# V cast while it is loaded, one clamp per half batch, first decay rows by small DMAs, and products in four 32-column tiles

## The chip, the cores and the metric

The kernel runs on one core of one Trainium2 chip. The metric is the device time in microseconds (us). TensorE (PE) multiplies, VectorE (DVE), ScalarE (ACT) and GpSimd (POOL) compute elementwise, SyncE (SP) only issues DMAs here; ACT and POOL issue some too.

## The reference

Eight batches of eight heads, 576 positions, head size 64; an attention with a decay (forget gate f), and after it a feed-forward net with a gated convolution along the sequence:

```python
log_f = np.log(np.clip(f, 0.0001, 1.0))
cum = np.cumsum(log_f, axis=-1)
scores = q @ k.T / sqrt(64) + cum[i] - cum[j]        # causal: j <= i
attn = softmax(scores);  x = attn @ v                # x: [8, 576, 512], heads side by side
h = relu(x @ w_in)                                   # [576, 1024]
conv = w0 * h[s-1] + w1 * h[s] + w2 * h[s+1]         # per channel
out = (h * sigmoid(conv)) @ w_out                    # [576, 512]
```

All inputs are fp32.

## The kernel before

A **half batch** (`hb`, 16 of them) is four heads. `load_qk` brings its q and k with a transposing DMA that treats each fp32 as two 16-bit numbers, so that the tile `qk` (four of them, a ring) has 128 rows: odd rows hold the upper halves (a bf16 each), even rows the lower halves, which are not wanted. Some even rows are used for the decay instead: with -8 cum in rows of k and of q and ones opposite, the decay comes out of the same matmul as the score. The other even rows must be zero. Three ways set the even rows:

- half batch 0: `clamp` (L203-206) clears the even rows by a VectorE multiply and add on the 16-bit patterns, four calls of 1152 columns; the decay is added by two more matmuls per score tile (L323, L325).
- half batches 1 to 5: `clamp`, four calls, sets ones and zeros; `rows_of` (L218) copies the decay rows by two DMAs on SP from `image`, a copy of them in DRAM.
- half batches 6 to 15: `fill` (L212) writes zeros by a DMA of 540 KB from `blank` in DRAM and then the rows by another. `constants` (L479) writes `blank` and part of `image` out of the buffer `qk3`, which POOL fills with zeros at the start (L263).

**Scores** (`tail_scores`, `diag_scores`, `off_scores`, all through L320): only blocks on or under the diagonal. ACT exponentiates them from PSUM (L332, L357, L347), POOL masks the diagonal blocks (L335, L360). The results are `pp` (two heads each) and `pt` (tail of four heads).

**Sums and products** (`sweep`, L368-382): ten pieces of the lower triangle for each of two heads, which write to two 64-column tiles of PE, 20 matmuls in all. With ones on the left (`sums`, L384) it gives the row sums, gathered for the eight heads of a batch in one PSUM tile; with V on the left (`pv`, L398) the product for two heads. `recip` (L389) turns the sums by a 32x32 transpose and takes reciprocals, `spread` (L394) turns them back for each pair of heads, and `norm` (L403) writes x in fp16 to `xt`, 128 rows for two heads.

**V** comes by five DMAs a batch on SP into an fp32 buffer `vf` (L223), and POOL casts it to fp16 in `va` (L231, two casts a half batch).

**The feed-forward part** of a batch: eight times `ffn1` (L410), `relu` on ACT (L418), two convolution steps on DVE (L424, L426), tanh on ACT (L429), the gate on DVE (L433); then `ffn2` (L435), copies out of PSUM (`evac`) and stores on SP. It overlaps with the attention of the following batches. `w_in` and `w_out` are cast by their DMAs on POOL (L500).

**The order** on every engine is fixed when the program is written: `Plan.play` (L36) runs tasks with given costs, keys, lags and buffer counts through a list schedule, and instructions are issued in that order. Engines then follow their own queue in order and wait on semaphores. SP's queue holds the loads of q and k, decay rows, V and stores; POOL's the masks, casts and weight loads. A load of half batch `hb` needs the buffer of `hb - 4`.

Of the kernel before, what the change touches and what calls it, by code (L numbers as in the profile page):

```python
# [114 lines left out]
def kernel(  # L115
# [11 lines left out]
    nc = tc.nc  # L127
# [14 lines left out]
    RING, NP, NPT, NVA, NVF, NHT, NU, NOB = 4, 6, 4, 4, 2, 4, 3, 3  # L142
    NCL = 6
# [8 lines left out]
    image = dpool.tile([4, 2, BH, S], BF16, name="image")  # L152
    blank = dpool.tile([60, 2 * HS], BF16, name="blank")
# [8 lines left out]
    lim = cpool.tile([128, 4], FP32, name="lim")  # L162
    lit = cpool.tile([128, 5], FP32, name="lit")
    lii = cpool.tile([128, 3], I32, name="lii")
    hix = cpool.tile([128, 4], I32, name="hix")
    hfx = cpool.tile([128, 4], FP32, name="hfx")
    sel_k = cpool.tile([128, 4], BF16, name="sel_k")
    sel_q = cpool.tile([128, 4, 128], BF16, name="sel_q")
    ones_h = cpool.tile([128, 4, 64], FP16, name="ones_h")
# [4 lines left out]
    vf_t = [cpool.tile([128, H, NKB, 64], FP32, name=f"vf{t}") for t in range(NVF)]  # L174
    va_t = [cpool.tile([128, HH, NKB, 64], FP16, name=f"va{t}") for t in range(NVA)]
# [5 lines left out]
    rt_t = [cpool.tile([128, 18, 4], FP32, name=f"rt{t}") for t in range(2)]  # L181
# [10 lines left out]
    plan = Plan({"ps": 4, "sc": 2, "mm": 2, "pv": 2, "p": NP, "pt": NPT, "pd": 2, "p3": 2, "st": 1, "rt": 2, "rb": 2, "xt": 2, "ht": NHT,  # L192
                 "u": NU, "hg": 2, "ob": NOB, "va": NVA, "vf": NVF, "qk": RING})
# [9 lines left out]
    def clamp(hb, p, side, eng):  # L203
        t = (stq_t, stk_t)[side][hb % RING].bitcast(U16)[:, 2 * p * S:2 * (p + 1) * S]
        eng.tensor_scalar(t, t, lim[:, 2 * side:2 * side + 1], lim[:, 2 * side + 1:2 * side + 2],  # L205
                          op0=ALU.mult, op1=ALU.add)
# [5 lines left out]
    def fill(hb):  # L212
        c = slice(hb * HH, (hb + 1) * HH)
        nc.sync.dma_start(even_rows(hb, 8, 60, 0, 2 * HS), blank)
        nc.sync.dma_start(even_rows(hb, 0, 4, 0, 2 * HS).rearrange("j (a x) -> j a x", a=2),
                          image[:, :, c, :].rearrange("j a h s -> j a (h s)"))

    def rows_of(hb):  # L218
        c = slice(hb * HH, (hb + 1) * HH)
        nc.sync.dma_start(even_rows(hb, 0, 1, 0, HS), image[0:1, 0, c, :].rearrange("j h s -> j (h s)"))  # L220
        nc.sync.dma_start(even_rows(hb, 2, 2, HS, 2 * HS), image[1:3, 1, c, :].rearrange("j h s -> j (h s)"))

    def load_v(b, t_load):  # L223
        vf = vf_t[slot[t_load, "vf"]]
        base = int(v.offset) + b * H * S * D
        for kb in range(NKB):
            n = 128 if kb < NKB - 1 else SL
            nc.sync.dma_start(vf[0:n, :, kb, :],
                              bass.AP(tensor=v.tensor, offset=base + kb * 128 * D, ap=[[D, n], [S * D, H], [1, D]]))

    def cast_v(t_load, t_cast, hb, part, eng):  # L231
        vf, va = vf_t[slot[t_load, "vf"]][:, HH * (hb % 2):HH * (hb % 2 + 1)], va_t[slot[t_cast, "va"]]
        if part == 0:
            eng.tensor_copy(va[:, :, 0:4, :], vf[:, :, 0:4, :])  # L234
        else:
            eng.tensor_copy(va[0:SL, :, 4, :], vf[0:SL, :, 4, :])


    nc.scalar.dma_start(fsb[0:BH], f.rearrange("b h s -> (b h) s"))
    nc.scalar.dma_start(fsb[BH:128], f.rearrange("b h s -> (b h) s"))  # L240
    nc.scalar.preload_act_table(AF.Ln)
    for p in range(2):
        for side in range(2):
            load_qk(0, 2 * p, 2, side)
    for side in range(2):
        load_qk(1, 0, 4, side)

    nc.gpsimd.iota(lii[:, 0:1], pattern=[[0, 1]], base=0, channel_multiplier=1)
    nc.gpsimd.iota(hix, pattern=[[1, 4]], base=0, channel_multiplier=0)
    nc.gpsimd.dma_start(cwrow, moe_conv_w)  # L250
    for t in range(RING - 1):
        nc.gpsimd.memset(stk_t[t][:, HS:HS + 64], 0.0)
    nc.gpsimd.memset(ones_h, 0.0)
    for c in range(4):
        for j in range(2):
            nc.gpsimd.memset(ones_h[:, c, 32 * j + c:32 * j + c + 1], 1.0)
    for t in range(NHT):
        nc.gpsimd.memset(ht_t[t][:, 0:1], 0.0)
        nc.gpsimd.memset(ht_t[t][:, S + 1:S + 2], 0.0)
    for t in range(NVA):  # L260
        nc.gpsimd.memset(va_t[t][64:128, :, NKB - 1, :], 0.0)
    make_identity(nc, ident)
    nc.gpsimd.memset(qk_t[3], 0.0)  # L263
    plus, minus = (t.bitcast(BF16)[0:BH, 0:S] for t in u_t[0:2])
    nc.gpsimd.memset(plus, 1.0)
    nc.gpsimd.memset(minus, -1.0)
    nc.vector.memset(one1, 1.0)
    nc.vector.tensor_scalar(lii[:, 1:2], lii[:, 0:1], 1, None, op0=ALU.bitwise_and)
    nc.vector.tensor_scalar(lii[:, 2:3], lii[:, 0:1], 63, None, op0=ALU.bitwise_and)
    nc.vector.tensor_copy(lit[:, 0:3], lii)  # L270
    nc.vector.tensor_copy(hfx, hix)
# [4 lines left out]
    nc.vector.tensor_scalar(lim[:, 3:4], lit[:, 0:1], 0.0, float(0xBF80), op0=ALU.is_equal, op1=ALU.mult)  # L276
    for side in range(2):
        nc.vector.tensor_copy(lim[:, 2 * side:2 * side + 1], lit[:, 1:2])
    nc.vector.tensor_scalar(sel_k, hfx, lit[:, 2:3], None, op0=ALU.is_equal)
    nc.vector.tensor_scalar(sel_q, hfx.unsqueeze(2).broadcast_to((128, 4, 128)), lit[:, 0:1], -1.0,  # L280
                            op0=ALU.is_equal, op1=ALU.mult)
# [7 lines left out]
    nc.gpsimd.dma_start(image[0, 0], kc[0:BH])  # L289
    nc.gpsimd.dma_start(image[1, 1], kc[0:BH])  # L290
    nc.gpsimd.dma_start(image[2, 1], kc[BH:128])
    clamp(0, 0, 1, nc.vector)
    clamp(0, 0, 0, nc.vector)
    clamp(0, 1, 1, nc.vector)
    clamp(0, 1, 0, nc.vector)

# [20 lines left out]
    def scores(ps, col, hb, h, k0, q0, n, m=128):  # L317
        tq, tk = stq_t[hb % RING], stk_t[hb % RING]
        o = ps[:, col:col + n]
        nc.tensor.matmul(o, tk[:, h * S + k0:h * S + k0 + 128], tq[:, h * S + q0:h * S + q0 + n],  # L320
                         start=True, stop=hb > 0)
        if hb == 0:
            nc.tensor.matmul(o[0:m], kc[:, k0:k0 + m], sel_k[:, h:h + 1].broadcast_to((128, n)),  # L323
                             start=False, stop=False)
            nc.tensor.matmul(o, sel_q[:, h, :], kc[:, q0:q0 + n], start=False, stop=True)  # L325

    def tail_scores(me, hb):
        for h in range(HH):
            scores(ps_t[slot[me, "ps"]], SL * h, hb, h, 512, 512, SL, m=SL)
# [38 lines left out]
    def sweep(ps, i, pp, pt, left_of, first, last):  # L368

        for x, (m, q0, n, kind) in enumerate(PIECES):  # L370
            for s in range(2):
                h = (2 * i + s) % HH
                if kind == "o":
                    c = 1024 * s + OFF[m] + q0 - 128 * (m + 1)
                    p = pp[:, c:c + n]
                elif kind == "d":
                    c = 2048 + 512 * s + 128 * m
                    p = pp[:, c:c + n]
                else:
                    p = pt[:, SL * h:SL * (h + 1)]  # L380
                nc.tensor.matmul(ps[64 * s:64 * (s + 1), AB + q0:AB + q0 + n], left_of(s, h, m), p,  # L381
                                 start=first and x in (0, 3), stop=last and x in (2, 9), skip_group_check=True)

    def sums(t_first, i, t_dg, t_tail):  # L384
        c = i % 4
        sweep(ps_t[slot[t_first, "ps"]], i, pp_t[slot[t_dg, "p"]], pt_t[slot[t_tail, "pt"]],
              lambda s, h, m: ones_h[:, c, :], c == 0, c == 3)

    def recip(t_first, me):  # L389
        st, rt = st_t[0], rt_t[slot[me, "rt"]]  # L390
        nc.vector.transpose(st, ps_t[slot[t_first, "ps"]][:, AB:AB + S])
        nc.vector.reciprocal(rt, st.rearrange("p (b t) -> p b t", t=32)[:, :, 0:4])

    def spread(t_rc, me, c):  # L394
        nc.vector.transpose(rb_t[slot[me, "rb"]].rearrange("p (b t) -> p b t", t=32),  # L395
                            rt_t[slot[t_rc, "rt"]][:, :, c:c + 1].broadcast_to((128, 18, 32)))

    def pv(me, i, t_dg, t_tail, t_va):  # L398
        va = va_t[slot[t_va, "va"]]
        sweep(ps_t[slot[me, "ps"]], i, pp_t[slot[t_dg, "p"]], pt_t[slot[t_tail, "pt"]],  # L400
              lambda s, h, m: va[:, h, m, :], True, True)
# [77 lines left out]
    def constants():  # L479
        for j in (1, 2):  # L480
            nc.gpsimd.dma_start(image[j, 0], plus)
        nc.gpsimd.dma_start(image[0, 1], minus)
        for a in range(2):
            nc.gpsimd.dma_start(image[3, a], qk_t[3][0:BH, 0:S])
        nc.gpsimd.dma_start(blank, qk_t[3][0:60, 0:2 * HS])

    add = plan.add
    t_cw = add({"PE": 1.0}, [], 2.6, lambda me: conv_weights(me), take=["ps"], lag=0.3)
    t_cwt = add({"DVE": 2.5}, [t_cw], 1.5, lambda me: conv_ratios(t_cw), give=[("ps", t_cw)])
# [205 lines left out]
```

## Time and profile before

| | us |
|---|---|
| median of 7 runs | 293.32 |
| lowest and highest | 292.33, 295.39 |
| the profiled execution, own time | 294.2 |
| its span, first to last instruction | 292.5 |
| PE busy | 243.8 |
| DVE busy | 240.0 |
| ACT busy | 197.9 |
| POOL busy | 96.1 |
| first matmul starts | 14.5 |
| first transpose of the sums (L391) starts | 44.3 |

Busy times are taken from the hardware profile of one execution. A group's row gives line, engine, operation, output and inputs, count, then busy us and mean ns of one, and after the second bar the idle time of the engine just before these instructions and what ended it. A wait row gives who waited for whom, total us, times and the longest. The DMA share counts the time of packets on all queues against 16 DMA engines; where packets of two queues overlap it can pass 1.

### The profile page before, as it was taken

How to read it: one execution, taken by the hardware profiler on the slowest of the kernel's cores; microseconds unless marked ns; L12 is line 12 of the kernel's file. 1: busy time of each engine (PE TensorE's matmuls, PEld its weight loads, DVE VectorE, ACT ScalarE, POOL GpSimd, SP SyncE). 2: the span in 40 equal slices, each digit the busy share in tenths (PEclk: the TensorE clock that was granted, in tenths of full speed). 3: DMA queues.
4: the chain of work that ended last, by engine and by line, in shares of the span. 5: the costliest groups of instructions: out<-in, count | busy, mean ns of one | idle time of the engine just before them, and what ended most of it. 6: DMA issues, size and time to landing. Idle time of an engine off the chain costs nothing.

```text
span 292.5 us, 6856 instructions
## 1 busy us (share of the span) xinstructions
PE 243.8 (83%) x2832; PEld 169.8 (58%) x2832; DVE 240.0 (82%) x322; ACT 197.9 (68%) x266; POOL 96.1 (33%) x133
## 2 busy tenths in 40 slices
PE   0099448597789799998988999999999999969990
PEld 0078336375655577576744875687568766854630
DVE  4852309979999888988998799989998999799871
ACT  1228535497656988886777878877887798626731
POOL 8625817136340327305246352125212121000000
PEclk9999959979999999999999999999999999999998
DMA  8997999999986999999999999999611001200404
GB/s 157 220 251 136 167 172 196 188 203 191 210 190 103 309 210 134 261 206 298 182 182 205 232 217 241 166 258 214 161 74 74 20 2 72 92 2 0 164 0 162
DMA packets 125683, 47.71 MB, mean 163 GB/s; under 512 B 117470, under 2 KB 120542, under 8 KB 124992
## 3 DMA queue, kind: packets, MB, share of 16 engines
q1 hardware_dynamic: 118852, 43.73, 71.6%
q0 software_dynamic: 6640, 3.25, 8.2%
q8 instruction: 22, 0.36, 0.5%
q10 hardware_dynamic: 160, 0.30, 0.4%
q14 instruction: 9, 0.07, 0.1%
HBM read 19.91 MB, written 10.58 MB: 104 GB/s over the span
## 4 chain that ended last, share of the span: by engine, by line
PE 46%; DVE 28%; ACT 9%; issue 5%; DMA 5%; POOL 4%; SPq 1%; ACTq 0%; POOLq 0%; DVEq 0%
PE ps L440 14%; PE ps L414 11%; PE ps L381 8%; PE ps L320 7%; DVE hg L433 6%; DVE u L426 5%; DVE u L424 5%; DVE xt L404 3%; ACT pd L357 3%; PE ps L454 3%; ACT pp L347 3%; DMA qk<-image 2%; DVE rb L395 2%; DMA rb<-in_f_dram 2%; ACT hg L429 2%
## 5 line engine op out<-in xcount | busy, mean ns | idle before, releaser
L320 PE MATMUL ps<-qk 128*128 128x128 bf16 (+3 forms) x576 | 63.6, 248 | 30.2 <-DVE qk L205 14.5
L414 PE MATMUL ps<-xt,w_in_f 128*128 128x288 f16 x512 | 72.2, 288 | 4.5 <-DVE xt L404 3.1
L347 ACT ACTIVATE pp<-ps 128x1024 f16<-128x1024 f32 x64 | 64.7, 1027 | 11.6 <-PE ps L320 9.6
L429 ACT ACTIVATE hg<-u,cw 128x576 f16<-128x576 f32 x64 | 49.5, 778 | 26.4 <-DVE u L426 25.9
L320 PEld LDWEIGHTS <-qk 128*128 128x128 bf16 x576 | 39.2, 101 | 42.7 <-issue 15.4
L433 DVE SCALAR_TENSOR_TENSOR hg<-hg,ht 128x576 f16<-128x576 f16 x64 | 54.8, 863 | 10.2 <-ACT hg L429 9.9
L360 POOL TENSOR_SCALAR_AFFINE_SELECT pp<-pd 128x1024 f16<-128x1024 f32 x32 | 38.6, 1206 | 74.4 <-ACT pd L357 74.4
L414 PEld LDWEIGHTS <-w_in_f 128*128 128x128 f16 x512 | 49.1, 98 | 22.8 <-issue 7.1
L424 DVE SCALAR_TENSOR_TENSOR u<-ht,cwt 128x576 f32<-128x576 f16 x64 | 57.2, 907 | 4.5 <-ACT ht L418 4.5
L426 DVE SCALAR_TENSOR_TENSOR u<-ht,cwt,u 128x576 f32<-128x576 f16 x64 | 59.3, 936 | 0.7
L440 PE MATMUL ps<-w_out_f,hg 128*128 128x512 f16 x224 | 51.7, 379 | 2.9 <-ACT pd L357 1.1
L418 ACT ACTIVATE ht<-ps 128x576 f16<-128x576 f32 x64 | 41.3, 656 | 16.9 <-PE ps L414 11.9
L357 ACT ACTIVATE pd<-ps 128x1024 f32<-128x1024 f32 x32 | 32.8, 1024 | 7.0 <-PE ps L320 4.0
L440 PEld LDWEIGHTS <-hg 128*128 128x128 f16 x224 | 21.6, 98 | 27.0 <-issue 2.6
L381 PE MATMUL ps<-pp,ones_h 128*64 128x128 f16 (+3 forms) x576 | 26.3, 242 | 1.5 <-ACT pp L347 0.9
L381 PE MATMUL ps<-pp,va 128*64 128x128 f16 (+3 forms) x576 | 24.8, 239 | 2.9 <-DVE xt L404 2.6
L381 PEld LDWEIGHTS <-ones_h 128*64 128x64 f16 x640 | 23.0, 112 | 6.3 <-issue 4.6
L381 PEld LDWEIGHTS <-va 128*64 128x64 f16 x640 | 22.6, 110 | 6.6 <-issue 5.2
L335 POOL TENSOR_SCALAR_AFFINE_SELECT pt<-p 128x256 f16<-128x256 f32 x16 | 10.0, 628 | 49.3 <-ACT p L332 49.3
L234 POOL CAST va<-vf 128x1024 f16<-128x1024 f32 x16 | 17.8, 1114 | 23.8 <-DMA vf<-in_v_dram 17.8
L395 DVE STREAM_TRANSPOSE rb<-rt 128x576 f32<-128x576 f32 x32 | 22.7, 745 | 0.0
L404 DVE TENSOR_TENSOR xt<-ps,rb 128x576 f16<-128x576 f32 x32 | 22.1, 725 | 0.0
(75 smaller groups left out, 166.5 us busy)
## 6 DMA issues: line engine op xcount, KB each, us to landing
vf<-in_v_dram SPq DMA_DIRECT2D x32, 256.0 KB, 6.0
out_dram<-ob SPq DMA_DIRECT2D x16, 512.0 KB, 2.8
qk<-blank SPq DMA_DIRECT2D x10, 540.0 KB, 5.3
vf<-in_v_dram SPq DMA_DIRECT2D x8, 128.0 KB, 4.9
w_in_f<-in_moe_w_in_dram POOLq DMA_DIRECT2D x4, 256.0 KB, 5.7
w_out_f<-in_moe_w_out_dram POOLq DMA_DIRECT2D x4, 256.0 KB, 7.3
out_dram<-ob SPq DMA_DIRECT2D x16, 64.0 KB, 2.1
blank<-qk POOLq DMA_DIRECT2D x1, 540.0 KB, 4.6
```

The lines of the kernel that those rows point to most:

```text
L320: nc.tensor.matmul(o, tk[:, h * S + k0:h * S + k0 + 128], tq[:, h * S + q0:h * S + q0 + n], start=True, stop=hb > 0)
L347: nc.scalar.activation(pp_t[slot[t_dg, "p"]][:, 1024 * s:1024 * (s + 1)], ps_t[slot[t_sc, "ps"]], AF.Exp, scale=SCALE)
L357: nc.scalar.activation(pd_t[slot[me, "pd"]], ps_t[slot[t_dg, "ps"]], AF.Exp, scale=SCALE)
L360: nc.gpsimd.affine_select(pp_t[slot[t_dg, "p"]][:, 2048:3072].rearrange("p (m j) -> p m j", j=128), pd_t[slot[t_ex, "pd"]].rearrange("p (m ...
L381: nc.tensor.matmul(ps[64 * s:64 * (s + 1), AB + q0:AB + q0 + n], left_of(s, h, m), p, start=first and x in (0, 3), stop=last and x in (2, ...
L414: nc.tensor.matmul(ps[:, MB + 288 * a:MB + 288 * (a + 1)], w_in_f16[:, cc, 128 * ff:128 * (ff + 1)], xt[:, cc, 288 * a:288 * (a + 1)], sta ...
L418: nc.scalar.activation(ht_t[slot[t_m1, "ht"]][:, 1:1 + S], ps_t[slot[t_m1, "ps"]][:, MB:MB + S], AF.Relu, scale=0.5)
L424: nc.vector.scalar_tensor_tensor(u, ht[:, 0:S], cwt[:, ff, 0:1], ht[:, 1:1 + S], op0=ALU.mult, op1=ALU.add)
L426: nc.vector.scalar_tensor_tensor(u, ht[:, 2:2 + S], cwt[:, ff, 1:2], u, op0=ALU.mult, op1=ALU.add)
L429: nc.scalar.activation(hg_t[slot[t_g0, "hg"]][:, ff, :], u_t[slot[t_u, "u"]], AF.Tanh, scale=cw[:, ff, 1:2])
L433: nc.vector.scalar_tensor_tensor(hv, hv, 1.0, ht_t[slot[t_m1, "ht"]][:, 1:1 + S], op0=ALU.add, op1=ALU.mult)
L440: nc.tensor.matmul(o, hg[:, ff, 128 * c:128 * (c + 1)], w_out_f16[:, ff, :], start=(ff == 0), stop=(ff == NFF - 1))
```

## The change

- **V.** `vf`, its loads on SP and the casts are gone. `load_v` issues five DMAs a batch on POOL that cast to fp16 while they load; `va` is now three buffers of a whole batch. The first batch's V is issued at the start, three blocks before the decay rows and two behind them.
- **Even rows.** `clamp` is one VectorE call per half batch over q and k (4608 columns), for every half batch, and sets ones, minus ones and zeros; half batch 0 has two calls of 2 x 1152. `fill`, `constants`, `blank` and the POOL fill of `qk3` are gone, and `image` keeps only its three planes of decay rows.
- **First decay rows.** `first_rows` copies the decay rows of half batch 0 straight from the tile `kc` by three small DMAs on POOL for each two heads. The two extra matmuls per score tile go.
- **Sums and products.** `sweep` takes four heads, each in a 32-column tile, 40 matmuls. `sums` runs once a half batch; `pv` twice, with the even and the odd columns of V (`e:64:2`). `recip` handles a half batch and includes the turn back. `xt` therefore holds four heads' even or odd columns in 128 rows, and `w_in` is loaded with rows `2p + e` to match, by two DMAs of 1 MB at the start.
- **Order.** f is loaded ahead of q and k, half on SP; k comes before q. Half batches 2 and 3 are loaded right behind the rows of half batch 1; the rows of half batch 2 follow all four loads. On PE the sums are made per half batch (those of half batch 0 stand ahead of half batch 1's scores); on DVE the clamp of half batch 2 stands behind the first norms. There are eight `pp` and five `pt` buffers for six and four. Plan costs, keys and start times are changed.

```diff
-    RING, NP, NPT, NVA, NVF, NHT, NU, NOB = 4, 6, 4, 4, 2, 4, 3, 3
-    NCL = 6
+    RING, NP, NPT, NVA, NHT, NU, NOB = 4, 8, 5, 3, 4, 3, 3
...
-    def clamp(hb, p, side, eng):
-        t = (stq_t, stk_t)[side][hb % RING].bitcast(U16)[:, 2 * p * S:2 * (p + 1) * S]
-        eng.tensor_scalar(t, t, lim[:, 2 * side:2 * side + 1], lim[:, 2 * side + 1:2 * side + 2],
-                          op0=ALU.mult, op1=ALU.add)
+    def clamp(hb, c0, c1):
+        t = qk_t[hb % RING].bitcast(U16)[:, 0:2 * HS].rearrange("p (a x) -> p a x", a=2)[:, :, c0:c1]
+        nc.vector.tensor_scalar(t, t, lim[:, 0:1], lim[:, 1:2], op0=ALU.mult, op1=ALU.add)
...
+    def first_rows(p):
+        c, t = slice(2 * p, 2 * p + 2), qk_t[0]
+        o = 2 * p * S
+        nc.gpsimd.dma_start(t[0:1, o:o + 2 * S], kc[c])
+        nc.gpsimd.dma_start(t[2:3, HS + o:HS + o + 2 * S], kc[c])
+        nc.gpsimd.dma_start(t[4:5, HS + o:HS + o + 2 * S], kc[BH + 2 * p:BH + 2 * p + 2])
+
+    def load_v(b, va, blocks=range(NKB)):
+        for m in blocks:
+            n = 128 if m < NKB - 1 else SL
+            nc.gpsimd.dma_start(va[0:n, :, m, :], v[b, :, 128 * m:128 * m + n, :].rearrange("h p d -> p h d"))
...
-    nc.scalar.dma_start(fsb[0:BH], f.rearrange("b h s -> (b h) s"))
+    nc.sync.dma_start(fsb[0:BH], f.rearrange("b h s -> (b h) s"))
...
-    nc.gpsimd.memset(qk_t[3], 0.0)
...
+    load_v(0, va_t[0], range(3))
...
+    clamp(0, 0, 2 * S)
+    first_rows(0)
+    clamp(0, 2 * S, 4 * S)
+    first_rows(1)
+    load_v(0, va_t[0], range(3, NKB))
+    nc.gpsimd.dma_start(image[0], kc[0:BH])
+    nc.gpsimd.dma_start(image[1], kc[0:BH])
+    nc.gpsimd.dma_start(image[2], kc[BH:128])
+    for x in range(2):
+        nc.gpsimd.dma_start(w_in_f16[:, 2 * x:2 * x + 2, :],
+                            moe_w_in[256 * x:256 * (x + 1), :].rearrange("(p e) ff -> p e ff", e=2))
...
-        if hb == 0:
-            nc.tensor.matmul(o[0:m], kc[:, k0:k0 + m], sel_k[:, h:h + 1].broadcast_to((128, n)),
-                             start=False, stop=False)
-            nc.tensor.matmul(o, sel_q[:, h, :], kc[:, q0:q0 + n], start=False, stop=True)
...
-                nc.tensor.matmul(ps[64 * s:64 * (s + 1), AB + q0:AB + q0 + n], left_of(s, h, m), p,
-                                 start=first and x in (0, 3), stop=last and x in (2, 9), skip_group_check=True)
+                nc.tensor.matmul(ps[32 * h:32 * (h + 1), AB + q0:AB + q0 + n], left_of(h, m), p,
+                                 start=x in (0, 3), stop=x in (2, 9), skip_group_check=True)
+
+    def sums(me, hb, t_dgs, t_tail):
+        sweep(ps_t[slot[me, "ps"]], hb, t_dgs, t_tail, lambda h, m: ones_h)
+
+    def recip(t_s, me):
+        st, rt, rb = st_t[0], rt_t[slot[me, "rb"]], rb_t[slot[me, "rb"]]
+        nc.vector.transpose(st, ps_t[slot[t_s, "ps"]][:, AB:AB + S])
+        nc.vector.reciprocal(rt, st.rearrange("p (b t) -> p b t", t=32)[:, :, 0:1])
+        nc.vector.transpose(rb.rearrange("p (b t) -> p b t", t=32), rt.broadcast_to((128, 18, 32)))
+
+    def pv(me, hb, e, t_dgs, t_tail, t_va):
         va = va_t[slot[t_va, "va"]]
...
+        sweep(ps_t[slot[me, "ps"]], hb, t_dgs, t_tail, lambda h, m: va[:, HH * (hb % 2) + h, m, e:64:2])
...
+        for g in {2: (2, 3), 3: ()}.get(hb, (hb,) if hb > 3 else ()):
+            for s in range(2):
+                t_ld[g, s] = add({"SP": 2.4}, old, 2.0 * g - 2.2 + 0.1 * s, lambda me, g=g, s=s: load_qk(g, 0, 4, s),
+                                 lag=2.5, dma=3.0, behind=[t_rows[1, 0]] if (g, s) == (2, 0) else [t_ld[g - 1 + s, 1 - s]])
...
+                t_vl[b] = add({"POOL": 4.0}, [], 4 * b + VKEY, lambda me, b=b: load_v(b, va_t[slot[me, "va"]]),
+                              take=["va"], lag=2.5, dma=5.2, behind=[t_vl[b - 1], t_ld[2 * b + (b == 1), 1]])
...
+            x = add({"DVE": 1.4}, [t_ld[hb, 0], t_ld[hb, 1]], base - 1.0, lambda me, hb=hb: clamp(hb, 0, HS))
+            fl = [add({"SP": 1.1}, [x], base - 0.8, lambda me, hb=hb: rows_of(hb), lag=2.5)]
...
-    order, _ = plan.play({"PE": 9.5, "ACT": 9.5, "DVE": 11.0, "POOL": 10.0, "SP": 8.0}, 13.0, 4.0)
+    order, _ = plan.play({"PE": 10.5, "ACT": 10.5, "DVE": 9.0, "POOL": 15.5, "SP": SP0}, 25.0, 5.0)
```

## The prediction

> **What bounds the kernel now.** I read the page's engine totals, the stretches of time, the waits and the groups of instructions, in that order. Two engines carry nearly the same load:
>
> ```profile
> PE 243.8 (83%) x2832; PEld 169.8 (58%) x2832; DVE 240.0 (82%) x322; ACT 197.9 (68%) x266; POOL 96.1 (33%) x133
> ```
>
> The stretches show where the rest is lost (columns: length, busy time of PE, weight loads, DVE, ACT, POOL, then clock, DMA share, GB/s):
>
> ```profile
> 24.00:40.00 16.00, 8.53 (x127) 6.39 (x125) 4.32 (x9) 8.78 (x10) 10.89 (x16) 0.93 0.84 143
> 33.00:40.00 7.00, 0.00 (x0) 0.00 (x0) 0.00 (x0) 0.36 (x1) 2.81 (x5) 0.83 1.13 157
> 190.00:219.00 29.00, 28.03 (x344) 19.82 (x342) 27.16 (x35) 23.96 (x34) 9.25 (x10) 1.00 0.75 178
> 264.00:286.00 22.00, 21.70 (x131) 10.41 (x128) 18.39 (x26) 12.77 (x19) 0.00 (x0) 1.00 0.15 54
> ```
>
> From 33 to 40 us PE and DVE do nothing. In a steady batch (29 us) PE has 28.0 and DVE 27.2: each is within two microseconds of being the bound, so the cheaper one buys little unless the other follows. The waits name the early hole:
>
> ```profile
> SPq L199 <- DMA blank<-qk: 9.0, 1, 9.0
> PE ps L320 <- DMA qk<-image: 11.4, 2, 8.1
> DVE st L391 <- PE ps L381: 15.2, 3, 12.8
> ```
>
> The load of the fourth half batch waits 9.0 us for the DMA that writes the blank rows out of that same buffer; the rows of half batch 2 stand behind it on SP; PE waits 8.1 us for them; the first transpose of sums on DVE (at 44.3) waits 12.8.
>
> **What the Trainium skill says.** "SBUF — State Buffer", Who interferes with whom: DVE in a two-port mode and GpSimd lock each other out for a whole instruction, and a DVE operation with two SBUF inputs contends with a GpSimd one that reads SBUF. The trace agrees; the first clip of f took 3.65 us beside a GpSimd fill, though L286 on the same 576 elements takes 0.46:
>
> ```profile
> 5.14 4.00 POOL L263 MEMSET qk<- 128x4672 bf16 x1
> 6.31 3.65 DVE L282 TENSOR_SCALAR rb<-rb 128x576 f32<-128x576 f32 x1 [3.26 <-DMA rb<-in_f_dram]
> ```
>
> "VectorE: DVE Perf Modes", Mode 4×_2P, gives four 16-bit elements a cycle: 1152 elements are then 0.30 us plus a fixed part; the trace's shortest is 0.48. "TensorE: Matmul & The Clock Gate", Part 3, says matmuls of different column tiles run side by side, starting about 4 ns apart; Part 1 has a floor of about 25 ns from start to start. The trace has pairs of 64-column tiles with the next sweep 30 ns after the pair began, 15 ns a matmul, so that floor does not hold across tiles:
>
> ```profile
> 220.36 0.20 PE L381 MATMUL ps<-pt,ones_h 128*64 128x64 f16 x2
> 220.39 0.83 PE L381 MATMUL ps<-pp,ones_h 128*64 128x128 f16 x18
> ```
>
> **The change, part by part.**
>
> Products and sums. Now 32 sweeps of sums and 32 of values, 20 matmuls each, 0.69 to 0.74 us (three take 2.21 in the chain). One head's pieces add up to 1600 columns, 0.67 us at the pace of 8 x 512 columns in 1.73 us (L440 in the chain): the sweep is at its stream. After: 16 + 32 sweeps of 40 matmuls, four heads abreast. Lower bound 0.69 (the same stream), upper 1.48 (40 at today's pace of 37 ns). I take 0.85, because the 15 ns above gives 40 x 15 = 0.60, under the stream. Per batch 6 x 0.85 = 5.1 for 8 x 0.72 = 5.8: PE falls from 28.0 to 27.3 (26.3 to 31.1 at the ends). Alone worth nothing while DVE has as much.
>
> Sums on DVE. These rows shrink:
>
> ```profile
> L395 DVE STREAM_TRANSPOSE rb<-rt 128x576 f32<-128x576 f32 x32 | 22.7, 745 | 0.0
> L391 DVE STREAM_TRANSPOSE st<-ps 128x576 f32<-128x576 f32 x8 | 6.2, 778 | 15.4 <-PE ps L381 15.2
> L392 DVE RECIPROCAL rt<-st 128x72 f32<-128x72 f32 x8 | 4.8, 603 | 0.3
> L205 DVE TENSOR_SCALAR qk<-qk,lim 128x1152 uint16<-128x1152 uint16 x24 | 15.9, 701 | 1.3 <-DMA qk<-in_q_dram 1.3
> ```
>
> Before 33.7 us; after 32 transposes at 0.74 and 16 reciprocals of 18 elements at 0.27 (an 8-element one, L309, takes 0.20, so 6.2 ns an element more): 28.0. Saves 5.7.
>
> Even rows. Half batches 6 to 15 have no clamp now; after, every one has one of 4608 elements: 1.2 us at four a cycle plus 0.2, 1.4 (upper bound 4 x 0.48 = 1.9). After 44 us today hold 12 clamps, 15.9 - 8.3 before = 7.6; the change puts 14 x 1.4 = 19.6 there, **plus 12.0 on DVE**. No other engine hides it. What it buys is the ten 540 KB blank fills (5.4 of 47.7 MB) and the 9.0 us wait.
>
> V. Sixteen pairs of casts leave POOL (28.6 us). Five DMAs a batch come onto POOL, 0.92 each by the w_out rows of like shape: 4.5 us a batch beside masks of 5.2, under the 29 us period. Masks queue behind them; sums wait for masks; POOL's slack of some 19 us covers it, and without that cover a mask is up to 4.5 late. SP loses 5 V issues a batch (4 to 8 us, mostly back-pressure), so q/k follow sooner. The transfer keeps its 4608 rows of 256 B a batch: by packet time from the page's queues 28 ns on the hardware queue, 58 on POOL's (8.2% of 16 x 292.5 us over 6640 packets, of 512 B and more), so 8 to 17 us of the 16 DMA engines a batch beside 16 for q/k and 2 to 3 for stores. At the upper end that is 35 and DMA sets the pace; I take the lower, since packets of two queues wait for each other and are counted twice (shares over 1). Casts read SBUF: with them the 24 three-operand calls of a batch take 0.88 to 0.91 for 0.72 back to back, 4.3 lost; from 219 us, without casts, about 3.0 (four delays of 0.75). Seven batches x 1.3 = 9 at most; I take 6, and 2 back for clamps meeting masks (the new two-port calls): **minus 4**.
>
> Start. The 4.0 us fill goes, so the clip is about 0.5: the row constants are ready near 10 instead of 13.3. But the first half batch's rows now cross a POOL DMA: clamp 0.75, three issues of 0.55 (three more for the second pair of heads), landing 2.1 (image<-u) to 4.4 (image<-kc): first scores at 14.5 to 17 against 14.5. Then one matmul for three, so ACT runs at 1.02 a call, not the 1.31 of today. POOL issues six row DMAs, two V, three image (done near 18), then w_in; image lands near 22, and SP, which holds half batch 1's rows and behind them all loads of 2 and 3, goes on then. Half batch 1 is exponentiated by 32 to 35, today 33.4: **nothing won there**. The gain comes next: sums of half batch 0 lie ahead of half batch 1 on PE, those of 1 need not wait for half batch 2's rows, and V and w_in are in by then. DVE's first uninterrupted work starts near 35 with 3 us of half batch 0 done, 32 in effect, against 44.3. Rows of half batch 2 now stand behind four loads on SP (4 x 2.7) and behind a clamp that follows the first norms on DVE: near 42, today 40.7, but then there are four first-layer groups to work on. Half batch 3 near 49, today 58.
>
> The sum. DVE from 44.3 to its last gate at 283.9: 239.6 us, busy 221.8 (sum of the stretches), idle 17.8. After: 221.8 + 12.0 - 5.7 - 4 = 224. Idle I leave at 18: less PE pressure, more waiting for early rows. 32 + 224 + 18 = 274, and 8.6 from last gate to end as now: span 282.6, against 292.5. The profiled run took 294.2, 1.7 around its span, and lies 0.9 over the median of 293.32: 282.6 + 1.7 - 0.9, about **283**.
>
> **The rivals.** A difference under 1% can't be told from none here.
> - *More* (0.20): casts were the whole extra delay (-3), clamps meet no mask (-2), DVE idle 12, since sums come per half batch (-6): 272. For it: PE idles 1.58 and DVE order spreads 7 us at the last batch's norms. Against: ACT has 24 of 29 too.
> - *Hidden* (0.12): the small row and image DMAs land late under a full queue (DMA share 1.2 in 16 to 24 us) and DVE starts at 41, nine later: 292. For it: 4.4 us landings. Against: the 9.0 wait is gone for certain.
> - *Slower* (0.18): the products don't overlap fourfold but issue at today's 37 ns: 1.48 a sweep. PE from 40 on has 225.7; minus 46 of sweeps, plus 45 x 1.48 = 67 (three run early): 246; from 33, with 14 idle and 6.5 of tail: 300 of span, 301. It decides from 1.32 a sweep on (equal to today's span), and shows only on PE. For it: twice the instructions per column, and value weights read with a step of two. Against: the 15 ns pairs.
> - My forecast, 277 to 289 (0.50).
>
> **How the numbers follow.** Faster by over 1%: forecast and *more*, and a little of *hidden*: 0.72. Slower: 0.18. Within 1%: 0.10. The range 271 to 298 leaves out half of *slower* and a quarter of *more*.
>
> **What would show it.** Sweeps of 40 in 0.7 to 1.0 us; clamps of 1.4 on DVE, 15 of them; the clip of f at 0.5; no PE hole from 33 to 40; first transpose of sums before 30; DVE above 27 us per 29. I am wrong if sweeps pass 1.3, if masks wait behind V on POOL, if V's packets cost 58 ns, or if DVE idles over 30 us for rows.

## The result and the profile after

The changed kernel takes 299.8 us in the median of 12 runs (297.2 to 303.0), beside 293.8 for the kernel before on the same chip. The ratio is 1.019, with a 95% interval of 1.016 to 1.023: **slower by 1.9%**, where 283 and a range of 271 to 298 had been predicted. Its profiled execution took 297.4 us, with a span of 295.7 (294.2 and 292.5 before), so the two traces show 3.2 of the 6 us between the medians. The ratios below are all to the kernel before, measured on the same chip at the same time as the version in question. They rest on executions within 1.5% of a version's fastest, which leaves 3 of 21 for e1 and 8 of 20 for e10 (over all of their runs the ratios are 1.015 and 0.999), and the traces of e1, e10 and e11 are from longer ones, so that their idle times may be too high.

The engine totals on the page of after:

```profile
PE 233.9 (79%) x3400; PEld 155.3 (53%) x3400; DVE 237.2 (80%) x322; ACT 198.2 (67%) x266; POOL 100.8 (34%) x116
```

Of PE, DVE and ACT none has got fuller: PE has 10 us less than before, DVE 3 less, ACT as much, and yet the span is 3 us longer. GpSimd, 5 us busier, is far from full. So the time is in waits. The stretches of after (length, then busy time of PE, weight loads, DVE, ACT, POOL, then clock, DMA share, GB/s) show where:

```profile
33.00:40.00 7.00, 4.40 (x132) 3.55 (x132) 4.25 (x6) 2.11 (x3) 7.00 (x8) 1.00 1.57 198
132.00:161.00 29.00, 25.03 (x321) 15.80 (x319) 25.20 (x30) 20.03 (x27) 10.68 (x10) 0.94 0.77 116
190.00:219.00 29.00, 26.68 (x363) 17.48 (x352) 27.10 (x35) 22.43 (x31) 6.06 (x6) 0.94 0.31 65
264.00:286.00 22.00, 21.66 (x133) 11.09 (x130) 15.18 (x21) 11.73 (x17) 0.00 (x0) 0.97 0.15 54
```

The hole from 33 to 40 us is gone: DVE works 4.25 of its 7 us there, before it worked none. But in a steady batch all three engines are now short of work together: from 132 to 161 us PE has 25.0, DVE 25.2 and ACT 20.0 of 29. In the same stretch of before each had more:

```profile
132.00:161.00 29.00, 25.74 (x276) 17.28 (x277) 26.87 (x31) 21.24 (x30) 13.95 (x14) 1.00 1.06 215
```

From 190 to 219 us PE falls from 28.0 to 26.7 and ACT from 24.0 to 22.4, while DVE keeps its 27. In the last stretch DVE falls from 18.4 to 15.2 of 22. From 44.3 us to its last gate DVE is idle for 29.4 us, before for 18.3. Of these 11 us, 4.2 lie ahead of 103 us, 2.8 between 103 and 248 (14.8 against 12.0), and 4.0 behind that.

The end of the normalised products of each batch (its last norm: L368, in before L404) tells when the lead was lost. Batch 0 ends at 39.0 us, before at 51.4, a lead of 12.4. Batch 2 has 107.9 against 113.1, batch 3 139.8 against 142.3. The last gate on DVE ends at 287.8 against 283.9. So the start won 12 us, and the rest lost 16.

The waits of after:

```profile
ACT ht L382 <- PE ps L378: 30.6, 28, 6.3
DVE u L388 <- ACT ht L382: 15.2, 10, 3.7
DVE hg L397 <- ACT hg L393: 9.7, 11, 3.6
DVE qk L198 <- DMA qk<-in_q_dram: 5.9, 3, 2.9
```

The first two of them in before:

```profile
ACT ht L418 <- PE ps L414: 11.9, 16, 1.6
DVE u L424 <- ACT ht L418: 4.5, 6, 1.0
```

Relu on ACT waited 11.9 us for the first layer's matmuls (now 30.6) and the first convolution step on DVE 4.5 us for relu (now 15.2). The fourth wait of after lies wholly ahead of 18 us. It is a chain, PE to ACT to DVE, that runs dry. One place where it does, the timeline of DVE, of PE and of ACT in after (start, length, instruction, in brackets the idle time ahead of it and its releaser):

```profile
135.26 2.36 DVE L198 TENSOR_SCALAR qk<-qk,lim 128x4608 uint16<-128x4608 uint16 x1
137.54 0.95 DVE L397 SCALAR_TENSOR_TENSOR hg<-hg,ht 128x576 f16<-128x576 f16 x1
138.41 1.41 DVE L368 TENSOR_TENSOR xt<-ps,rb 128x576 f16<-128x576 f32 x2
139.75 1.46 DVE L198 TENSOR_SCALAR qk<-qk,lim 128x4608 uint16<-128x4608 uint16 x1
144.33 0.82 DVE L388 SCALAR_TENSOR_TENSOR u<-ht,cwt 128x576 f32<-128x576 f16 x1 [3.12 <-ACT ht L382]
```

```profile
139.21 3.41 PE L404 MATMUL ps<-w_out_f,hg 128*128 128x512 f16 x8 [2.72 <-DVE xt L368]
142.46 2.12 PE L378 MATMUL ps<-xt,w_in_f 128*128 128x288 f16 x16
```

```profile
143.64 0.66 ACT L382 ACTIVATE ht<-ps 128x576 f16<-128x576 f32 x1 [6.29 <-PE ps L378]
```

At 137.5 DVE makes the last gate of a batch, and at 138.4 the last norms of the next. PE had waited 2.7 us for DVE. In PE's written order a group of the second layer (L404) stands next, and behind it the first group of the first layer (L378) of the next batch. Only after these can ACT make a relu (6.3 us idle) and DVE a convolution step (3.1 us idle). DVE had nothing of the old batch left and nothing of the new one yet. The eight matmuls of L404 after the pause take 3.41 us; the next eight, at 144.4, take 1.89. The clock column shows the difference between the two:

```profile
139.20:142.60 3.40, 3.39 (x10) 1.25 (x10) 2.01 (x2) 0.00 (x0) 3.40 (x4) 0.54 1.15 87
144.40:146.20 1.80, 1.80 (x11) 0.84 (x9) 1.76 (x3) 0.65 (x1) 0.00 (x0) 1.00 1.71 220
```

From 139 to 142 us the granted clock is 0.50. Two more such stretches of 3.4 us follow in after, near 190 us (behind a pause of PE of 1.9 us) and near 262 (behind pauses of 2.1 and 1.0 us); before has none between 62 us and its last gate. Each makes PE's work some 1.7 us longer (an estimate: half of 3.4). They are not what empties the chain in the main: e6 below, another order of after with a clock of 1.00 from 103 to 248 us, lets DVE idle for 12.8 us there, against 14.8 in after.

### The profile page after: what moved, and what is told of

It is laid out like the page before. It is cut to its first block, busy times and chain, and to the rows that moved or that the text cites. A ratio compares the mean times of both kernels' runs of the same rounds, so it can differ in the third digit from the quotient of the medians.

```text
span 295.7 us, 7921 instructions
## 1 busy us (share of the span) xinstructions
PE 233.9 (79%) x3400; PEld 155.3 (53%) x3400; DVE 237.2 (80%) x322; ACT 198.2 (67%) x266; POOL 100.8 (34%) x116
## 3 DMA queue, kind: packets, MB, share of 16 engines
q0 software_dynamic: 42272, 7.07, 32.6%
## 4 chain that ended last, share of the span: by engine, by line
DVE 42%; PE 34%; ACT 9%; issue 6%; POOL 3%; DMA 2%; SPq 2%; DVEq 0%; ACTq 0%
PE ps L378 11%; PE ps L404 11%; DVE u L390 10%; DVE u L388 9%; DVE hg L397 8%; PE ps L293 5%; DVE xt L368 4%; DVE qk L198 4%; PE ps L351 4%; DVE st L359 3%; DVE rb L361 2%; ACT hg L393 2%; DMA qk<-in_q_dram 2%; ACT pp L316 2%; PE ps L409 2%
## 5 line engine op out<-in xcount | busy, mean ns | idle before, releaser
L293 PE MATMUL ps<-qk 128*128 128x128 bf16 (+3 forms) x576 | 62.1, 250 | 27.1 <-DMA qk<-kc 10.0
L378 PE MATMUL ps<-xt,w_in_f 128*128 128x288 f16 x512 | 74.4, 294 | 5.5 <-DVE xt L368 5.2
L388 DVE SCALAR_TENSOR_TENSOR u<-ht,cwt 128x576 f32<-128x576 f16 x64 | 57.5, 908 | 15.2 <-ACT ht L382 15.2
L329 POOL TENSOR_SCALAR_AFFINE_SELECT pp<-pd 128x1024 f16<-128x1024 f32 x32 | 39.7, 1241 | 78.1 <-ACT pd L326 77.8
L382 ACT ACTIVATE ht<-ps 128x576 f16<-128x576 f32 x64 | 41.6, 650 | 31.9 <-PE ps L378 30.6
L378 PEld LDWEIGHTS <-w_in_f 128*128 128x128 f16 x512 | 49.5, 100 | 24.7 <-issue 8.4
L293 PEld LDWEIGHTS <-qk 128*128 128x128 bf16 x576 | 39.6, 102 | 43.6 <-issue 15.2
L404 PE MATMUL ps<-w_out_f,hg 128*128 128x512 f16 x224 | 54.8, 391 | 6.4 <-DVE xt L368 3.3
L397 DVE SCALAR_TENSOR_TENSOR hg<-hg,ht 128x576 f16<-128x576 f16 x64 | 49.1, 775 | 9.8 <-ACT hg L393 9.7
L219 POOL DMA_DIRECT2D va<-in_v_dram x40 | 38.6, 984 | 0.5 <-issue 0.4
L404 PEld LDWEIGHTS <-hg 128*128 128x128 f16 x224 | 21.8, 100 | 30.2 <-issue 6.5
L198 DVE TENSOR_SCALAR qk<-qk,lim 128x4608 uint16<-128x4608 uint16 (+1 forms) x17 | 26.1, 1533 | 8.3 <-DMA qk<-in_q_dram 5.9
L351 PE MATMUL ps<-pp,va 128*32 128x128 f16 (+3 forms) x1152 | 27.5, 243 | 3.7 <-ACT pp L316 1.8
L351 PEld LDWEIGHTS <-va 128*32 128x32 f16 x1280 | 23.0, 99 | 9.7 <-issue 7.3
L368 DVE TENSOR_TENSOR xt<-ps,rb 128x576 f16<-128x576 f32 x32 | 23.1, 748 | 4.5 <-PE ps L351 4.1
L429 ACT COPY ob<-ps 128x1024 f32<-128x1024 f32 (+1 forms) x23 | 18.0, 789 | 11.8 <-PE ps L404 9.8
L351 PE MATMUL ps<-pp,ones_h 128*32 128x128 f16 (+3 forms) x576 | 15.4, 244 | 6.4 <-ACT pp L316 6.2
```

Of the source, the lines that this page charges most:

```text
L219: nc.gpsimd.dma_start(va[0:n, :, m, :], v[b, :, 128 * m:128 * m + n, :].rearrange("h p d -> p h d"))
L293: nc.tensor.matmul(ps[:, col:col + n], tk[:, h * S + k0:h * S + k0 + 128], tq[:, h * S + q0:h * S + q0 + n], start=True, stop=True)
L329: nc.gpsimd.affine_select(pp_t[slot[t_dg, "p"]][:, 2048:3072].rearrange("p (m j) -> p m j", j=128), pd_t[slot[t_ex, "pd"]].rearrange("p (m ...
L351: nc.tensor.matmul(ps[32 * h:32 * (h + 1), AB + q0:AB + q0 + n], left_of(h, m), p, start=x in (0, 3), stop=x in (2, 9), skip_group_check=True)
L378: nc.tensor.matmul(ps[:, MB + 288 * a:MB + 288 * (a + 1)], w_in_f16[:, cc, 128 * ff:128 * (ff + 1)], xt[:, cc, 288 * a:288 * (a + 1)], sta ...
L382: nc.scalar.activation(ht_t[slot[t_m1, "ht"]][:, 1:1 + S], ps_t[slot[t_m1, "ps"]][:, MB:MB + S], AF.Relu, scale=0.5)
```

## The experiments

Two things can be behind this. **Load**: the clamps of half batches 6 to 15 are simply more work on DVE. **Order**: the written order of the instructions keeps PE, ACT and DVE waiting for each other (the "ring" of the expectations). **V** on GpSimd is a third. In the table, "DVE busy" and "idle" are of the profiled execution, from 44.3 us to the last gate.

| version | ratio to before | 95% interval | DVE busy | DVE idle |
|---|---|---|---|---|
| before | 1 | | 221.3 | 18.3 |
| after | 1.019 | 1.016 to 1.023 | 214.1 | 29.4 |
| e1_after_blank_fills | 0.998 | 0.993 to 1.004 | 204.1 | 44.1 |
| e2_no_v_loads | 0.996 | 0.993 to 0.999 | 214.7 | 24.8 |
| e3_replanned | 0.971 | 0.966 to 0.976 | 213.9 | 18.4 |
| e4_before_all_clamped | 1.012 | 1.008 to 1.016 | 230.6 | 12.1 |
| e5_clamps_twice | 1.056 | 1.048 to 1.065 | 233.6 | 26.1 |
| e6_prices_only | 1.001 | 0.998 to 1.004 | 213.3 | 27.3 |
| e7_key_only | 0.982 | 0.974 to 0.990 | 217.5 | 17.8 |
| e8_before_replanned | 1.015 | 1.012 to 1.018 | 218.5 | 25.5 |
| e9_replanned_no_v | 0.968 | 0.960 to 0.977 | 214.0 | 16.3 |
| e10_before_no_blank_wait | 0.988 | 0.984 to 0.992 | 213.7 | 25.4 |
| e11_after_late_fills | (0.993) | none | 202.6 | 38.1 |
| e12_replanned_late_fills | 0.955 | 0.947 to 0.963 | 201.8 | 26.4 |
| e13_before_key_45 | 1.014 | 1.008 to 1.020 | 214.5 | 30.7 |
| e14_after_key_50 | 1.010 | 1.005 to 1.015 | 213.0 | 31.3 |

### The order alone

Each task of the plan has a key: of the tasks of an engine that are ready, the plan writes the one with the lowest key first. A higher key for the first layer puts it later in the order.

```diff
-        k1 = 4 * b + 4.5
+        k1 = 4 * b + 5.5
...
-            x = add({"DVE": 1.4}, [t_ld[hb, 0], t_ld[hb, 1]], base - 1.0, lambda me, hb=hb: clamp(hb, 0, HS))
+            x = add({"DVE": 1.62}, [t_ld[hb, 0], t_ld[hb, 1]], base - 1.0, lambda me, hb=hb: clamp(hb, 0, HS))
...
-        t_rb = add({"DVE": 1.75}, [t_s], ks - 0.1, lambda me, t_s=t_s: recip(t_s, me), take=["rb"], give=[("ps", t_s)])
+        t_rb = add({"DVE": 1.85}, [t_s], ks - 0.1, lambda me, t_s=t_s: recip(t_s, me), take=["rb"], give=[("ps", t_s)])
...
-            u0 = add({"DVE": 0.8}, [y, t_cwt], key + 0.2, lambda me, x=x, ff=ff: conv(x, me, ff, 0), take=["u"])
+            u0 = add({"DVE": 0.91}, [y, t_cwt], key + 0.2, lambda me, x=x, ff=ff: conv(x, me, ff, 0), take=["u"])
```

In the same way u1 gets 0.91 for 0.8, and the sums and both products 0.69 for 0.87.

> The changed kernel, same instructions, but the plan gets the durations that the profile of after shows (convolution steps 0.91 for 0.8, clamp 1.62 for 1.4, sums and turn 1.85 for 1.75, sweeps 0.69 for 0.87), and the first layer of the feed-forward part is keyed one unit later (5.5 for 4.5), so another order comes out. Order theory: VectorE idle falls from 28 to 14 to 18 us, 285 to 291. Load theory: VectorE has the same 224 us to do behind the start and the same collisions, 297 to 301.

The same instructions in another order take 286.6 us, 0.971. This is the order theory's number, and far from the load theory's. DVE's busy time is unchanged (213.9 for 214.1), its idle time is 11 us shorter. The steady part gives as much: from 103 to 248 us DVE now idles 3.7 us for 14.8 (ahead of that 9.7 for 6.6, behind it 4.9 for 7.9). The stretches of this version, its waits, and its batch boundary on DVE:

```profile
132.00:161.00 29.00, 28.50 (x450) 19.15 (x452) 28.61 (x37) 25.10 (x35) 10.81 (x11) 1.00 0.95 155
190.00:219.00 29.00, 26.29 (x383) 17.73 (x380) 28.14 (x36) 23.33 (x32) 5.21 (x6) 1.00 0.19 58
```

```profile
DVE u L388 <- ACT ht L382: 7.4, 10, 3.1
DVE hg L397 <- ACT hg L393: 5.9, 8, 1.7
```

```profile
134.15 1.39 DVE L397 SCALAR_TENSOR_TENSOR hg<-hg,ht 128x576 f16<-128x576 f16 x2
135.46 1.42 DVE L368 TENSOR_TENSOR xt<-ps,rb 128x576 f16<-128x576 f32 x2
136.79 0.81 DVE L388 SCALAR_TENSOR_TENSOR u<-ht,cwt 128x576 f32<-128x576 f16 x1
137.51 1.47 DVE L198 TENSOR_SCALAR qk<-qk,lim 128x4608 uint16<-128x4608 uint16 x1
138.90 0.96 DVE L390 SCALAR_TENSOR_TENSOR u<-ht,cwt,u 128x576 f32<-128x576 f16 x1
```

DVE fills 28.6 of 29 us. The last norms of a batch (135.5) are followed at once by a convolution step (136.8), of the batch still in work, and no bracket of idle time stands in the five lines. Two changes were made at once here, so each was run alone.

> The changed kernel, the plan's prices left as they are, only the first-layer key 5.5 for 4.5. If the key is the cause: 287 to 292. If the prices are: 296 to 301. If both are needed, each alone stays 4 us or more above the replanned version's 286.6.

> The changed kernel, order made with the measured durations (as in the replanned version), first-layer key left at 4.5. Order theory, if the plan's too cheap VectorE calls are the cause: most of the 13 us of the replanned version, 287 to 292. If the key is the cause: within 3 us of after, 297 to 302.

The key alone gives 0.982, most of the gain, and takes 11.6 us off DVE's idle time. The prices alone give 1.001, between their two cases, and DVE still idles 27 us. Together they give 0.971.

What the key does can be read off the written order of PE: how many groups of the first layer, counted over all batches, stand ahead of the first group of the second layer of batches 0, 1, 2 and so on. In before it is 12, 19, 27, 35, 43, 51: three or four groups of the next batch come first, since each batch has eight. In after it is 8, 16, 24, 32, 40, 48: **none does**. On DVE all eight gates of a batch stand ahead of the last norm of the next. With the key at 5.5 it is 11, 19, 27, 35, 43, 51 again. So in after these batches no longer overlap in the feed-forward part, and the chain is refilled behind each boundary: there the first convolution step waits 1.9, 0.4, 3.1, 1.0, 1.0 and 3.0 us for relu, 10.5 of the 15.2 us in the list of waits. To see whether this overlap or the low key itself costs, the key was changed in both kernels, in before (shown) to 4.5 and in after to 5.0:

```diff
-        k1 = 4 * b + 5.0
+        k1 = 4 * b + 4.5
```

> The kernel before with the changed kernel's key (4.5 for 5.0) and nothing else. In the written order, 11 first-layer groups then stand ahead of the first second-layer group of batch 0, and 17, 27, 33, 43 and 49 ahead of those of the next batches (12, 19, 27, 35, 43, 51 in before; 8, 16, 24, 32, 40, 48 in after): most of the overlap of two batches stays. If lost overlap is what costs, 1.00 to 1.015. If the low key by itself costs what it costs in after, 1.025 to 1.045.

> The changed kernel with the key of before (5.0 for 4.5) and nothing else. Its written order has 8, 18, 26, 34, 43, 48 first-layer groups ahead of the first second-layer group of each batch, between after (8, 16, 24, 32, 40, 48) and the key 5.5 (11, 19, 27, 35, 43, 51). Overlap theory: between the two times, 0.99 to 1.01. If the choice of key in the change was the whole fault, before's key restores it: 0.975 to 0.985.

Both lie at an edge of what the overlap theory had: after with the old key 1.010, between its two neighbours, though its trace idles as much (31.3) as after; before with the low key 1.014, at the top of its case. The wait of DVE that rises most in before with the low key is the same as in after (4.5 us with the key at 5.0):

```profile
DVE u L424 <- ACT ht L418: 18.0, 20, 3.7
```

So a first layer that is ordered too early costs there too, although 17 instead of 19 groups, 33 instead of 35, are ahead: the count of overlapping groups is not the whole measure. The prices alone (e6) say the same: that order has 8, 16, 25, 32, 40, 48 groups ahead, hardly more than after, and is still 1.8% faster. And the old key would not have saved after: of the three keys tried only 5.5 does. So it is shown that the written order costs the time; that the missing overlap is what is wrong with it is the likeliest reading, but not proven. Last, before with prices from its own profile:

```diff
-            u0 = add({"DVE": 0.8}, [y, t_cwt], key + 0.2, lambda me, x=x, ff=ff: conv(x, me, ff, 0), take=["u"])
+            u0 = add({"DVE": 0.92}, [y, t_cwt], key + 0.2, lambda me, x=x, ff=ff: conv(x, me, ff, 0), take=["u"])
...
-            gates[b, ff] = add({"DVE": 0.8}, [th], key + 0.1, lambda me, x=x, g0=g0, ff=ff: gate(x, g0, ff),
+            gates[b, ff] = add({"DVE": 0.86}, [th], key + 0.1, lambda me, x=x, g0=g0, ff=ff: gate(x, g0, ff),
```

u1 gets 0.92 too, sums and products 0.71 for 0.75.

> The kernel before, order made with the durations of its own profile (convolution steps 0.92, gate 0.86 for 0.8, sweeps 0.71 for 0.75), keys as they are. If the order of before has the same fault, it gains as much as after did, 12 us or more, to 283, and the change is worth nothing at equal planning; if its order already fits (VectorE idles 17.8 us there, of which most lies ahead of 72 us), it gains 0 to 4 us, 291 to 296, and the parts of the change are worth their 8 us or so once the order fits them.

1.015, slower, outside of both cases. So truer prices alone don't make a better order of before. But the premise that its order fits was misread: of the 18.3 us that DVE idles there, only 1.6 lie ahead of 72 us, and 12.0 between 103 and 248, where the replanned version has 3.7. A later key, which gave after most of its gain, was not tried in before. What the change is worth when both kernels have an order that fits is therefore not shown.

### The clamps

```diff
-            x = add({"DVE": 1.4}, [t_ld[hb, 0], t_ld[hb, 1]], base - 1.0, lambda me, hb=hb: clamp(hb, 0, HS))
+            x = add({"DVE": 1.4}, [t_ld[hb, 0], t_ld[hb, 1]], base - 1.0,
+                    lambda me, hb=hb: (clamp(hb, 0, HS), clamp(hb, 0, HS) if hb > 5 else None))
```

> The changed kernel with the clamp of half batches 6 to 15 made twice in a row, order unchanged: ten more VectorE calls of 1.4 to 1.6 us, plus 15. Load theory: all of them count, about 1.019 + 0.05 = 1.07 of the kernel before (315 us). Order theory: VectorE idles 28 us behind the start, but mostly because its own late gates hold up PE and ACT, so an added call there is in the ring and counts too, while slack elsewhere takes some: plus 8 to 15, 1.047 to 1.07. A result under plus 6 would say that VectorE's calls are not in the ring at all.

Ten clamps more cost 0.037 of 295 us, 11 us (8 to 14 by the two intervals). The group's row in the trace (busy, mean ns, idle ahead of it) is 14.3 us above the 26.1 of after:

```profile
L198 DVE TENSOR_SCALAR qk<-qk,lim 128x4608 uint16<-128x4608 uint16 (+1 forms) x27 | 40.4, 1497 | 11.3 <-DMA qk<-in_q_dram 7.6 <-DMA qk<-in_k_dram 3.3
```

About three quarters count. The ratio lies in the order theory's range, 1.047 to 1.07, and below the load theory's 1.07. In the kernel before, one clamp for each half batch instead of the blank fills:

```diff
-    NCL = 6
+    NCL = NHB
...
-            for p in range(2 if hb < NCL else 0):
-                for s in range(2):
-                    cl.append(add({"DVE": 0.6}, [t_ld[hb, s]], base - 1.0 + 0.1 * (2 * p + s),
-                                  lambda me, hb=hb, p=p, s=s: clamp(hb, p, s, nc.vector)))
+            cl.append(add({"DVE": 1.4}, [t_ld[hb, 0], t_ld[hb, 1]], base - 1.0, lambda me, hb=hb: clamp_all(hb)))
```

> The kernel before with one part of the change alone: one clamp of 4608 columns for each half batch from 1 on, no blank fill for 6 to 15 (the fill's constants and the zero fill of the fourth buffer stay, so the start is as before). VectorE behind the start gets 14 x 1.6 for 7.6 us, so plus 14. Load theory: all of it counts, 304 to 309. Order theory: VectorE has 17.8 us of waits behind 44 us that take a part, 297 to 303.

1.012: 3.5 us, at the bottom of the order theory's case. DVE is busy 9.3 us longer and idles 6 us less: before, with overlapping batches, had room for most of it. Then the other way, the fills put back into after. The first try wrote the blank rows early (GpSimd issues five more DMAs and the 540 KB one while half batch 1 is masked):

```diff
+            if hb == 1:
+                t_const = add({"POOL": 5.5}, [t_mask[1]], 1.05, lambda me: constants(), lag=2.5, dma=2.0)
...
+            else:
+                fl = [add({"SP": 1.5}, [t_ld[hb, 0], t_ld[hb, 1], t_const], base - 1.5, lambda me, hb=hb: fill(hb), lag=3.0,
+                          dma=2.2)]
```

> The changed kernel, with the even rows of half batches 6 to 15 set as before by the blank fill from DRAM, so that ten clamps of about 1.62 us leave VectorE (its zeros come from the second gate buffer, so no load waits for them). Load theory (VectorE is simply fuller by the clamps): 16 us less on VectorE, nearly all of it won, 284 to 288. Order theory (the written order, made with VectorE calls priced 10% under what they take, keeps PE, ACT and VectorE waiting for each other): the order is made by the same plan, so most of the 16 us comes back as VectorE idle time, 295 to 299.

The ratio is 0.998, at the edge of what the order theory had. But it rests on three runs, and in its trace the norms of batch 1 ended at 85.7 us instead of 73.4, so it is no clean measure of the clamps. The second try made the constants wait for `t_mask[4]`, near 50 us, with after's order and with the prices and key of the replanned version:

> The changed kernel with blank fills for half batches 6 to 15 in place of their clamps once more, but the blank rows are written to DRAM only near 50 us, so that the start stays as in after; same plan prices. Ten clamps of 1.62 us leave VectorE. At the price of a VectorE microsecond in the doubled clamps (11 for 15) this gives 12 less, 0.98. If VectorE's load counts fully, 0.965. If it only turns to idle time in the ring, 1.00 or more.

> The same with the measured durations in the plan and the key 5.5. VectorE has 16 us less than in the replanned version (0.971). If VectorE is the bound there: 0.925 to 0.94. If PE is next (232 us busy, 28 of 29 us a batch in before): 0.95 to 0.965. If the fills' 5.4 MB cost as much as the clamps: 0.97.

In after's order the four runs lay at 285.4, 292.4, 293.0 and 294.6 us, beside 294.9 for before, too wide for an interval; the profiled one has 11.5 us less on DVE, and 8.7 of them came back as idle time (38.1). In the replanned order it is 0.955, 280.7 us, the fastest of all. It has 12 us less on DVE than the replanned version, and 4.8 us of that show. This is the second case, PE next, if any: PE is busy 230.6 of its 281.0 us of span, but 28.3 of every 29 from 161 to 219 us.

### V, and the early start

```diff
-                              lambda me, b=b: load_v(b, va_t[slot[me, "va"]])
+                              lambda me, b=b: load_v(b, va_t[slot[me, "va"]]) if b < 3 else None
```

> The changed kernel, but V of batches 3 to 7 is not loaded (the buffers keep the V of earlier batches, so this part of the work is left out): 25 casting DMAs of 1024 rows less on GpSimd and in the DMA engines. V theory (masks late behind V on GpSimd, full DMA engines): 4 to 8 us less than 299.8, so 292 to 296. Load and order theory: within 1.5 us of 299.8.

> The replanned version without the loads of V for batches 3 to 7 (left out, earlier V is used again). Without replanning this took 2.3% off. V theory (GpSimd issues and packets cost by themselves): again 2% or more, 0.950 or less of the kernel before. Order theory (a late mask only hurts where the ring of waits has no slack): under 1%, 0.962 to 0.971.

Without V's later loads after is 2.3% faster (0.996), which was the V theory's number. In the replanned order the same edit gives nothing that can be told (0.968 against 0.971, with intervals that overlap). So V cost time in the one order and was hidden, GpSimd issue and packets, in the other.

```diff
-    nc.gpsimd.memset(qk_t[3], 0.0)
+    zero = hg_t[1].rearrange("p f s -> p (f s)").bitcast(BF16)
+    nc.gpsimd.memset(zero, 0.0)
...
-        nc.gpsimd.dma_start(blank, qk_t[3][0:60, 0:2 * HS])
+        nc.gpsimd.dma_start(blank, zero[0:60, :])
```

> The kernel before with one thing changed: the zeros for the blank rows come from the second gate buffer and no longer from the fourth q/k buffer, so the load of half batch 3 doesn't wait 9 us for them; the other loads and the order stay. If an early lead lasts to the end: rows of half batch 2 land 5 to 8 us earlier, the first transpose of sums starts near 38, 286 to 290 (0.97 to 0.985). If the order eats it, as it ate 12 us in after: within 1%.

The early hole of before by itself is worth between nothing and 3.5 us: 0.988 on eight runs, less than the case of a lasting lead had, and 0.999 on all twenty. In its trace the first transpose of sums starts at 35.9 us for 44.3, 8.4 earlier; DVE idles 7 us longer behind 44.3. An early start is mostly given back here as well.

## Why the prediction was wrong

The sum was start, plus DVE's work, plus DVE's idle time, plus the tail. Term by term, with DVE's work counted from the first uninterrupted transpose (35.5 us) to the last gate (287.8):

| | forecast | measured |
|---|---|---|
| start of uninterrupted work | 35 | 35.5 |
| DVE busy behind it | 221 (224, less 3 done early) | 222.6 |
| DVE idle | **18** | **29.7** |
| last gate to end | 8.6 | 7.9 |
| span | 282.6 | 295.7 |

11.7 of the 13.1 us that are missing in the span are the idle time. (The profiled execution lies 2.4 us below the median; the forecast had put it 0.9 above. That part of the miss is in no trace.) **The step that failed is "Idle I leave at 18: less PE pressure, more waiting for early rows".** The idle time of before belonged to an order in which two batches overlap. The diff of the key (5.0 to 4.5) and of the plan was left at "are changed", and the order that comes out of it was not looked at where one batch follows another. With an order that fits (e3), idle behind its first uninterrupted transpose at 37.0 is 18.6 us, and 37.0 + 221.0 + 18.6 + 8.1 gives its span of 284.7: the other terms were right. That the 18 comes back there is partly luck, since it lies elsewhere: 9.7 us ahead of 103 us, where before had 2.4, and 3.7 from 103 to 248, where before had 12.0. The recorded sign "DVE idles over 30 us for rows" came close in size, not in kind: behind 35.5 us no idle time of DVE ends with a DMA.

- *Sweeps.* Taken at 0.85, they ran at the lower bound, 0.69 from one to the next. The rival *slower* had the sign of the result, but not its reason. In the timeline of PE in after, two products of the first batch begin their large groups 0.69 us apart:

```profile
35.34 0.83 PE L351 MATMUL ps<-pp,va 128*32 128x128 f16 x33
36.03 0.83 PE L351 MATMUL ps<-pp,va 128*32 128x128 f16 x33
```

- *Sums on DVE.* 28.0 forecast, 29.2 measured: the transposes take 0.775 each, for 0.74.
- *Clamps.* Forecast at 1.4, 15 of them took 24.3 us, 1.62 each, 3 us more in all. Most take 1.47, but one beside a mask (1.09 us of L329 within it) takes 2.36: the line at 135.26 above. This agrees with the Trainium skill, "SBUF — State Buffer", Who interferes with whom. The 2 us that had been set aside for meeting masks match the 2.3 us above 15 x 1.47 partly by luck: 0.9 are this clamp, and 1.15 are one of 2.62 at 76 us, which meets no mask but GpSimd's issues of V.
- *Casts gone.* The three three-operand groups of the feed-forward part fell from 171.3 to 164.5 us, 6.8 for a forecast of 6, most of it (54.8 to 49.1) in the gates. The casts were not taken out alone.
- *V on POOL.* Forty issues took 38.6 us, 0.98 each for 0.92; hidden, as e9 shows, where the order has slack. The packets of GpSimd's queue come to 36.5 ns (32.6% of 16 x 295.7 us over 42272), between the bounds of 28 and 58.
- *Start.* Clip of f 0.88 for 0.5, row constants ready at 8.6 for 10, first scores at 15.5 within 14.5 to 17: near the forecast. What it was thought to bring, one for one, it doesn't: e10 gets at most 3.5 us for 8.4.
- *DVE as the bound.* A microsecond on DVE was taken at its full price. By the clamps' rows it was worth 0.76 in after (e5: 10.9 for 14.3), 0.4 in before (e4: 3.5 for 8.4) and 0.3 in the replanned order (e12: 4.8 for 16.1), each give or take 0.2 by the intervals. In e4 and e12 the blank fills change as well.
- *The rival on the slower side* was put on the wrong engine. A rival "the written order no longer overlaps two batches" was missing; its signs were all in the two listings of instructions.

Still open is how much each of the other parts (the four-tile products, the casting V) is worth alone at a fitting order, and whether before gains as much as after did from a later key; neither was run.

## What to carry to other kernels

Where engines run a written order, the idle time of a profile belongs to that order: after an edit that makes a new one, count at the boundary of two stages what of the next stage stands ahead of the last work of this one, on each engine, before any saving is added up. A change that makes instructions cheaper should be timed with its order fitted again, since a 4.8% difference can lie in the order alone. And take a part away once in a bad and once in a good order: V cost 2.3% in one and nothing in the other.

## What was not expected of the hardware

A sweep of 40 matmuls over four 32-column tiles takes 0.69 us, 17 ns a matmul. It is as fast per sweep as the 20 matmuls over two 64-column tiles before, so the floor of 25 ns from start to start that the prediction quoted does not hold across tiles here either: in the sweep at 35.3 us the matmuls of the four heads mostly start 3 to 4 ns apart.

After a pause of 2.7 us PE was granted a clock of 0.50 for 3.4 us (1.00 just ahead of that): eight matmuls of 512 columns took 3.41 us, and soon after 1.89. This pause so cost PE twice, which was not in the sum.
